# Two layers of chunked attention with a memory and a gated FFN on one core: weight loads moved to SyncE's queue, and the instruction orders built with other margins

## The chip, the cores and the metric

One core of one Trainium2 chip runs the whole program. The metric is device microseconds (us) of one launch, on that core. The kernel before took 537.57 us (median of three runs, 535.77 to 541.40).

## What is computed

The reference works on x of 2048 tokens by 512 channels, in bf16. It does the same two steps twice, with the same weights:

```
x = x + A(layernorm(x), wq, wk, wv, wo, beta)
x = x + B(layernorm(x), w1, w3, w2)
```

A is attention with 32 heads of 16 channels. The 2048 tokens are cut into four segments of 512. Inside a segment every head does causal softmax attention. Beside that, each segment reads a memory that the earlier segments have written:

```
num = phi(qs) @ M ; den = phi(qs) @ z ; a_mem = num / (den + 1e-6)
o   = g * a_mem + (1 - g) * a_dot
M  += phi(ks)^T @ vs ; z += sum over tokens of phi(ks)      # phi(t) = t + 1 for t > 0, else exp(t)
```

with g = sigmoid(beta) of the head, and o @ wo closes the step. B is `(silu(x @ w1) * (x @ w3)) @ w2` with 1376 hidden channels.

## The kernel before, in words

**Segments.** The kernel has eight segment passes, numbered g = 0 to 7 (g = 4 * layer + segment, L949 to L979). A pass normalises its 512 tokens (`layer_norm`), projects q, k and v (`project`), reads the memory (`phi`, `memory_read`; not in segment 0), does the attention (`attention`), writes the memory (`memory_update`; not in segment 3), multiplies by wo and adds (`out_proj`, L878 and L882), normalises again and runs the gated FFN (`ffn`: gate and up products at L909, the down product at L937). All activations and weights stay in SBUF.

**Attention.** The scores of a pass come in 20 units (`unit_list`). A unit is four matmuls of 512 score columns on four row groups of TensorE (L765, "R" work), one exponential on ScalarE (L774, 2048 columns at once, or two of 1024 in pass 0), and causal masks on GpSimd (L787). Later the products with v follow (L813, "C" work), an eviction to `xs` (L448 or L449), a DMA transpose `xg<-xs` on SyncE's queue (L825), the division by the row sums (`normalise`: `rd` at L849 and L848, `og` at L858 or L861), and a DMA transpose `W<-og` (L870) that feeds wo. Pass 0 is done in two halves of 256 tokens, each with its own attention, wo product and second normalisation. Everything else on TensorE is "F" work: projections, wo, FFN.

**Transposes.** The layer norm writes `xn` (L553), and SyncE's queue transposes it into the ring `W` (L557). Transposes of phi(k) (L645) and of `og` go the same way. SyncE's queue carries all 188 DMA transposes.

**The order of the work.** No engine order is written by hand. `Sched` takes all operations with their buffers, priorities and modelled costs, and plays through the program once at build time (`schedule`, L122). For each engine it works out the time s at which each candidate could start: its inputs' modelled ends plus a latency (`_lat`, L117), and the engine's own free time. Candidates within LOOK of the earliest compete by priority. What is picked is appended to that engine's list. The lists are emitted as they are, with semaphore waits (`finalize`, `emit`), so every engine is strictly in order on the chip: where an input is later than the plan thought, the engine stands still, and everything behind it in its list too. A DMA queue is such an engine as well (`sp`, and the issue slots of `act` and `pool`). `gates` hold a candidate back until some other operation is placed in the plan, without a semaphore; `after` adds a real wait.

**The loads.** L493 to L500 issue x tiles 0 to 3, wq, wk and beta from the queues of SyncE and ScalarE. `second_loads` (L502) issues wv from SyncE's queue after the second transpose of pass 0, and x tiles 4 to 7 from GpSimd's queue after the last `lnrs`. `late_loads` (L513) issues the rest from GpSimd's queue, each behind one score unit n of pass 0 (`late`, L510): x tiles 8 to 11 behind unit 1, wo behind 3, w1 and w3 in halves of 688 KB behind 5, 7, 9 and 11, w2 behind 13, 15 and 17, x tiles 12 to 15 behind 18. At the start TensorE runs 28 matmuls on zeros (`WARM`, L475).

Of the kernel before, what the change touches and what calls it, by code (L numbers as in the profile page):

```python
# [8 lines left out]
P = 128  # L9
# [52 lines left out]
class Sched:  # L62
# [53 lines left out]
    @staticmethod  # L116
    def _lat(d, e):  # L117
        if d.dmaq is not None:
            return LAT + (DMA_SLACK if e == "pe" else 0.0)
        return LAT_SAME if d.eng == e else LAT  # L120

    def schedule(self):  # L122
# [15 lines left out]
        xpose_free = 0.0  # L138
# [7 lines left out]
        while left:  # L146
            best = None
            for e in ENGS:
# [3 lines left out]
                for op in avail[e]:  # L152
                    s = max(tf, op.avail_at) if op.gates else tf
# [32 lines left out]
                for s, op in cands:  # L186
                    if s > lim:
                        continue
# [11 lines left out]
            if best is None:  # L200
                held = {}
                for op in self.ops:
                    for b in op.bufs:
                        if b.slot is not None and b.left:
                            held[id(b)] = b
                for b in held.values():
                    print(b.pool.name, b.slot, [(u.name, u.prio) for u in b.users if not u.issued][:3])
                raise RuntimeError("stuck: " + "; ".join(
                    "%s %s" % (op.name, [b.pool.name for b in op.bufs + op.hold if b.slot is None]) for e in ENGS for op in avail[e][:4]))
# [30 lines left out]
            else:  # L240
                if op.mode == "T":
                    x0 = max(s, xpose_free)
                    op.end = x0 + lat + 0.8 * min(max(dma_free - x0, 0.0), 3500.0)
                    xpose_free = x0 + occ
# [3 lines left out]
                else:  # L248
                    x0 = max(s + 700.0, dma_free)
                    dma_free = x0 + op.size / (LOAD_RATE if op.dmaq == "pool" else 300.0)  # L250
# [97 lines left out]
def o_pool(n, per=1.04):  # L348
    return ("pool", 170.0 + per * n, 170.0 + per * n)
# [9 lines left out]
def build(nc, A_x, A_wq, A_wk, A_wv, A_wo, A_beta, B_w1, B_w3, B_w2, out):  # L359
# [81 lines left out]
    def dmaT(fn, **k):  # L441
        return S.add([("sp", 1290.0, 2500.0)], fn, dmaq="sp", mode="T", **k)
# [26 lines left out]
    WARM = 7  # L469
# [32 lines left out]
    def second_loads(first):  # L502
        xt = [op for op in S.ops[first:] if op.name == "xT"]
        ldw("sp", wv_sb, A_wv, "wv", CP + 3, gates=[xt[1]])
        rs = [op for op in S.ops[first:] if op.name == "lnrs"][-1]
        dma("pool", x_tok[:, 4:8, :], xv[:, 4:8, :], 524288, prio=CP + 4, writes=[("x", 4 + j) for j in range(4)], name="ldx",
            gates=[rs], after=[rs])
# [4 lines left out]
    def late_loads():  # L512
        late(x_tok[:, 8:12, :], xv[:, 8:12, :], 524288, 1, [("x", 8 + j) for j in range(4)], "ldx")  # L513
        late(wo_sb[:], A_wo.rearrange("(g p) f -> p g f", p=P), 524288, 3, ["wo"], "ldwo")
        for a in range(2):
            for n, (t, src, key) in enumerate(((w1_sb, B_w1, "w1"), (w3_sb, B_w3, "w3"))):
                late(t[:, 2 * a:2 * a + 2, :], src[256 * a:256 * a + 256, :].rearrange("(g p) f -> p g f", p=P), 704512,
                     5 + 4 * a + 2 * n, [key + str(a)], "ld" + key)
        for a in range(2):
            late(w2_sb[:, 5 * a:5 * a + 5, :], B_w2[640 * a:640 * a + 640, :].rearrange("(t p) d -> p t d", p=P), 655360,  # L520
                 13 + 2 * a, ["w2%d" % a], "ldw2")
        late(w2_sb[0:96, 10, :], B_w2[1280:1376, :], 98304, 17, ["w22"], "ldw2")
# [10 lines left out]
    def layer_norm(s, name, prio, gates=(), fine=False, part=(0, LT), dst=None):  # L533
# [4 lines left out]
        for i in tiles:  # L538
# [3 lines left out]
            dve(lambda e, i=i: e.bn_aggr(ln_r[st.slot][:, i, 6:8], ln_r[st.slot][:, i, 0:6]), 40, reads=[(st, 0, i)],  # L542
                writes=[(st, 1, i)], bufs=[st], prio=prio, name="bnag")
        for a, b in ([(0, 2), (2, 4)] if fine else [part]):
            dve(lambda e, a=a, b=b: e.tensor_scalar(ln_r[st.slot][:, a:b, 8], ln_r[st.slot][:, a:b, 7], 1e-5, None, op0=ALU.add), 20,
                reads=[(st, 1, i) for i in range(a, b)], writes=[(st, 2, i) for i in range(a, b)], bufs=[st], prio=prio, name="lnve")
            pool(lambda e, a=a, b=b: e.tensor_tensor(ln_r[st.slot][:, a:b, 9], ln_r[st.slot][:, a:b, 8], mhalf[:, a:b], ALU.pow), 800,  # L547
                 reads=[(st, 2, i) for i in range(a, b)] + ["mhalf"], writes=[(st, 3, i) for i in range(a, b)], bufs=[st],
                 prio=-1e5 + prio, name="lnrs")
        for i in tiles:  # L550
            tt = 4 * s + i
            xn = new("xn")
            S.add([o_dve(512, False, 1.05)], lambda e, i=i, tt=tt, xn=xn: e.tensor_scalar(  # L553
# [73 lines left out]
    def phi(src, t, dst, dt_, prio, gates=()):  # L627
        for hf in range(2):
# [8 lines left out]
                1024, mode=1.53, reads=[(x, 0), (dst, hf)], writes=[(dst, hf)], bufs=[x, dst], prio=prio, name="phmin")  # L637
# [4 lines left out]
    def memory_update(g, z, pkb):  # L642
# [5 lines left out]
        for hf in range(2):  # L648
            B = new("B")

            def fn(e, hf=hf, B=B):
# [15 lines left out]
                480, reads=[("macc", hf), "bdm"], writes=[(mb, hf)], bufs=[mb], prio=g + 0.3, name="mblk")  # L667
        mstate["mb"] = mb

    def memory_read(g, pqb):  # L670
# [4 lines left out]
        def fn(e):  # L675
            o = None
            for G in range(NCG):
                for i in range(LT):
# [9 lines left out]
                                      gg[:, 0, :][:, None, :].to_broadcast([P, LT, H]), ALU.mult), 128,  # L688
# [139 lines left out]
    def normalise(g, z, part, G, xg, oms):  # L828
# [20 lines left out]
        dve(lambda e: e.reciprocal(rd_r[rd.slot][:, 0, 0:n], sums()), 6.2 * n, reads=[(xg, 0), (xg, 1)], writes=[(rd, 0)],  # L849
            bufs=[xg, rd], prio=pr, name="rd")  # L850
        dve(scaled, n, reads=[(rd, 0), "g1"], writes=[(rd, 1)], bufs=[rd], prio=pr, name="rdg")
        ogv = lambda: og_r[og.slot][:].rearrange("p t (a e d) -> p t a e d", e=2, d=DH)
        for k in range(2):
# [9 lines left out]
            S.add([o_dve(95 * nt), o_pool(64 * nt, 2.25)], fn, reads=[(xg, 0), (xg, 1), (rd, 1)], writes=[(og, k)],  # L863
# [10 lines left out]
    def out_proj(s, g, z, part):  # L874
        for i in range(*part):
            B = new("B")
            for G in range(NCG):
                pe(lambda e, i=i, G=G, B=B: e.matmul(bank(B), ot_r[z.ot.slot][:, G, 128 * i:128 * i + 128], wo_sb[:, G, :],  # L878
                                                     start=(G == 0), stop=(G == NCG - 1)), MM512,
                   reads=[(z.ot, a, i) for a in range(NCG)] + ["wo"], writes=[(B, 0)], bufs=[B, z.ot],  # L880
# [5 lines left out]
    def ffn(s, g, X, part, last=False):  # L886
# [43 lines left out]
        for i in range(t0, t1):  # L930
            B = new("B")
            tt = 4 * s + i
            for ft in range(NFT):
# [5 lines left out]
                    MM512, reads=[(h, 0), "w2%d" % (ft // 5)], writes=[(B, 0)], bufs=[B, h], prio=base + step * n, gates=[prev],  # L939
# [9 lines left out]
    for layer in range(2):  # L949
        for s in range(NS):  # L950
# [16 lines left out]
            if g == 0:  # L967
                later_constants([units[(0, 2)]])
# [47 lines left out]
```

## Time and profile before

| | |
|---|---|
| median of the runs | 537.57 us (535.77 to 541.40) |
| profiled execution, its own time | 541.07 us |
| its span, first to last instruction | 539.2 us, so 1.87 us lie around it |
| mean granted TensorE clock | 0.953 |
| score unit on ScalarE (2048 columns) | 1.88 us, 140 of them |
| gate or up product (512 columns, L909) | 0.388 us latency each, 560 of them |

In the rows, a time is in us from the start of the span; "SPq" is SyncE's DMA queue; the bracket at the end of a timeline row is the idle time of that engine before the instruction and what ended it. PEclk is the granted TensorE clock, 1.00 being full speed. A row of a window gives the busy time of each engine in it, with the number of instructions in round brackets.

### The profile page before, as it was taken

Reading aid. Unit: us, or ns where it says so; the run is one execution under the profiler, and the core shown is the slowest. Engines: PE = TensorE matmul, PEld = TensorE weight load, DVE = VectorE, ACT = ScalarE, POOL = GpSimd, SP = SyncE. Lnnn points to the kernel's source line nnn. Section 1 sums busy time; section 2 is a strip of 40 time slices with the busy share of each in tenths; the row PEclk is TensorE's granted clock in tenths of the full one; section 3 lists DMA queues with packets and bytes.
Section 4 is the critical chain, followed back from the end, with each engine's and each line's share of the span. In section 5 each row is a group of like instructions: output and inputs, shape, how many; then the busy total and the mean of one; then the engine's idle time right before and its main releaser. Section 6 shows DMA issues by size and latency. Waiting matters only on the chain.

```text
span 539.2 us, 10460 instructions
## 1 busy us (share of the span) xinstructions
PE 502.7 (93%) x4180; PEld 218.9 (41%) x4180; DVE 412.1 (76%) x821; ACT 387.2 (72%) x331; POOL 239.1 (44%) x349
## 2 busy tenths in 40 slices
PE   7875997989999999999889999889999999999997
PEld 3431343355455344333334343333333434444443
DVE  5486498888797889677977796989877947777473
ACT  2896687979988989788978798967897877113130
POOL 2685333456554556454534475546654554100000
PEclk9985597989999999999979999999998999999999
DMA  7577653143222314322442034423421141030101
GB/s 189 129 198 173 154 82 78 30 71 80 40 60 42 68 30 89 70 59 51 52 96 50 10 71 68 73 46 56 82 46 34 36 103 41 21 78 1 39 1 39
DMA packets 107200, 36.91 MB, mean 68 GB/s; under 512 B 101296, under 2 KB 105392, under 8 KB 107152
## 3 DMA queue, kind: packets, MB, share of 16 engines
q1 hardware_dynamic: 104640, 29.12, 28.2%
q0 software_dynamic: 1552, 6.32, 4.2%
q8 instruction: 33, 0.54, 0.5%
q10 hardware_dynamic: 960, 0.79, 0.4%
q14 instruction: 15, 0.12, 0.1%
HBM read 8.43 MB, written 2.10 MB: 20 GB/s over the span
## 4 chain that ended last, share of the span: by engine, by line
PE 67%; DVE 16%; DMA 10%; ACT 3%; issue 1%; POOL 1%; SPq 1%; ACTq 0%; DVEq 0%
PE psall L909 26%; PE psall L937 12%; PE psall L765 7%; PE psall L597 6%; PE psall L813 6%; PE psall L878 5%; DMA xg<-xs 3%; PE psall L592 3%; DMA W<-xn 2%; ACT e L774 2%; DMA W<-og 2%; DVE ln L540 1%; DVE xn L553 1%; DVE W L449 1%; DVE W L634 1%; DVE W L636 1%
## 5 line engine op out<-in xcount | busy, mean ns | idle before, releaser
L774 ACT ACTIVATE e<-psall 128x2048 bf16<-128x2048 f32 (+1 forms) x180 | 300.7, 1697 | 57.0 <-PE psall L765 55.3
L787 POOL TENSOR_SCALAR_AFFINE_SELECT e<-e 128x512 bf16<-128x512 bf16 x256 | 164.0, 660 | 165.7 <-ACT e L774 165.5
L909 PE MATMUL psall<-W,w 128*128 128x512 bf16 (+3 forms) x792 | 176.3, 364 | 4.7 <-DVE gp L922 2.4
L909 PEld LDWEIGHTS psall<-W,w 128*128 128x128 bf16 (+1 forms) x792 | 75.2, 102 | 83.6 <-issue 13.8
L920 ACT ACTIVATE th<-psall 128x512 bf16<-128x512 f32 (+2 forms) x89 | 51.6, 591 | 56.9 <-PE psall L909 56.8
L937 PE MATMUL psall<-w,h 128*128 128x512 bf16 (+1 forms) x352 | 85.8, 380 | 0.0
L922 DVE SCALAR_TENSOR_TENSOR gp<-th,psall 128x512 bf16<-128x512 bf16 (+2 forms) x89 | 59.4, 676 | 17.1 <-ACT th L920 16.8
L926 DVE SCALAR_TENSOR_TENSOR h<-gp,psall 128x512 bf16<-128x512 bf16 (+1 forms) x89 | 59.6, 674 | 10.2 <-PE psall L909 9.9
L813 PE MATMUL psall<-e,va 128*32 128x256 bf16 (+3 forms) x1088 | 46.5, 310 | 4.5 <-POOL e L787 2.9
L765 PE MATMUL psall<-W 16*128 16x256 bf16 (+3 forms) x544 | 42.8, 305 | 8.5 <-ACT e L774 7.3
L937 PEld LDWEIGHTS psall<-w,h 128*128 128x128 bf16 (+1 forms) x352 | 32.5, 98 | 38.5 <-issue 4.9
L540 DVE BATCH_NORM_STATS2 ln<-x_tok 128x6 f32<-128x512 bf16 x64 | 43.0, 682 | 1.3 <-DMA x_tok<-in_A_x_dram 0.9
L765 PE MATMUL psall<-W,km 32*128 32x256 bf16 (+3 forms) x544 | 43.1, 307 | 0.4 <-ACT e L774 0.4
L942 DVE TENSOR_TENSOR x_tok<-psall,x_tok 128x512 bf16<-128x512 f32 x32 | 21.9, 685 | 24.8 <-PE psall L937 24.8
L449 DVE CAST xs<-psall 128x512 bf16<-128x512 f32 x56 | 36.7, 681 | 5.4 <-PE psall L813 5.2
L592 PE MATMUL psall<-wv,W 128*128 128x512 bf16 x128 | 36.5, 404 | 4.4 <-DMA wv<-in_A_wv_dram 1.7
L449 DVE CAST W<-psall 128x512 bf16<-128x512 f32 x44 | 29.8, 681 | 11.0 <-PE psall L597 10.9
L597 PE MATMUL psall<-W,wq 128*128 128x512 bf16 (+1 forms) x144 | 35.8, 359 | 1.9 <-DMA W<-xn 1.8
L813 PEld LDWEIGHTS psall<-e,va 128*32 128x32 bf16 x1088 | 24.8, 101 | 28.0 <-POOL e L787 8.2
L597 PE MATMUL psall<-W,wk 128*128 128x512 bf16 (+1 forms) x144 | 36.2, 357 | 0.0
L858 POOL TENSOR_TENSOR og<-xg,rd 128x256 bf16<-128x256 bf16 x33 | 24.6, 750 | 25.4 <-DVE rd L848 21.9
L553 DVE TENSOR_SCALAR xn<-x_tok,ln 128x512 bf16<-128x512 bf16 x64 | 32.5, 531 | 3.6 <-POOL ln L547 3.5
(61 smaller groups left out, 426.9 us busy)
## 6 DMA issues: line engine op xcount, KB each, us to landing
w<-in_B_w_dram POOLq DMA_DIRECT2D x4, 688.0 KB, 5.1
out_dram<-x_tok SPq DMA_DIRECT2D x16, 128.0 KB, 1.7
x_tok<-in_A_x_dram POOLq DMA_DIRECT2D x3, 512.0 KB, 5.6
km<-W SPq DMA_DIRECT2D x24, 64.0 KB, 2.4
w<-in_B_w_dram POOLq DMA_DIRECT2D x2, 640.0 KB, 5.7
W<-xn SPq DMA_TRANSPOSE x64, 2.5
xg<-xs SPq DMA_TRANSPOSE x64, 2.4
W<-og SPq DMA_TRANSPOSE x36, 2.4
```

The lines of the kernel that those rows point to most:

```text
L449: return e.tensor_copy(dst(), src())
L592: fn = lambda e, cg=cg, G=G, B=B, st=st, sp_=sp_: e.matmul(bank(B), xa_r[X.slot][:, cg, 128 * G:128 * G + 128], wv_sb[:, cg, :], start=st, ...
L597: fn = lambda e, cg=cg, G=G, B=B, st=st, sp_=sp_, w=w, a=a, W=W, c0=c0: e.matmul(bank(B)[:, W * a:W * a + W], w[:, cg, 128 * G:128 * G + 1 ...
L765: o = e.matmul(S4[:, sps(pg), c:c + n], kk[32 * pg:32 * pg + r, G, 128 * j:128 * j + 128], q_r[z.q.slot][32 * pg:32 * pg + r, G, 128 * t1 ...
L774: act(lambda e, N=N, ebuf=ebuf, pgs=pgs, sps=sps: e.activation(e_r[ebuf.slot][:, pgs[0]:pgs[-1] + 1, 0:N], S4[:, sps(pgs[0]):sps(pgs[-1]) ...
L787: pool(lambda e, ebuf=ebuf, c=c: e.affine_select(e_r[ebuf.slot][:, :, c:c + 128], e_r[ebuf.slot][:, :, c:c + 128], pattern=[[0, 4], [1, 128]],
L813: o = e.matmul(bank(X)[32 * pg:32 * pg + 32, base + W - n:base + W], va_r[z.va.slot][:, j, h:h + 32], e_r[eb.slot][:, pg, c:c + n], start= ...
L909: prev = pe(lambda e, i=i, cg=cg, ft=ft, B=B, w=w: e.matmul(bank(B)[0:width(ft), W * i:W * i + W], w[:, cg, 128 * ft:128 * ft + width(ft)] ...
L920: act(lambda e, fw=fw, NW=NW, B=B, th=th: e.activation(th_r[th.slot][0:fw, 0:NW], bank(B)[0:fw, 0:NW], ACT.Tanh, scale=0.5), NW, reads=[(B ...
L922: dve(lambda e, fw=fw, NW=NW, B=B, th=th, gp=gp: e.scalar_tensor_tensor(gp_r[gp.slot][0:fw, 0:NW], th_r[th.slot][0:fw, 0:NW], 1.0, bank(B) ...
L926: dve(lambda e, fw=fw, NW=NW, B=B, gp=gps[fg], h=hs[fg]: e.scalar_tensor_tensor(h_r[h.slot][0:fw, 0:NW], gp_r[gp.slot][0:fw, 0:NW], 0.5, b ...
L937: prev = pe(lambda e, ft=ft, fw=fw, B=B, h=h, c=c: e.matmul(bank(B), h_r[h.slot][0:fw, c:c + 128], w2_sb[0:fw, ft, :], start=(ft == 0), st ...
```

## The change

Constants of the planner and its modelled latency:

```diff
-LAT = 60.0
-LAT_SAME = 30.0
-DMA_SLACK = 500.0
-LOAD_RATE = 210.0
+LAT = 150.0
+LAT_SAME = 80.0
+DMA_SLACK = 800.0
+LOAD_RATE = 280.0
...
-LOOK = {"pe": 90.0, "act": 150.0, "dve": 40.0, "pool": 20.0, "sp": 20.0}
+R_SLACK = 0.0
+SLACK = {"pe": 120.0, "act": 0.0, "dve": 200.0, "pool": 60.0, "sp": 0.0}
+LOOK = {"pe": 90.0, "act": 100.0, "dve": 20.0, "pool": 20.0, "sp": 20.0}
...
-            return LAT + (DMA_SLACK if e == "pe" else 0.0)
+            return LAT + (DMA_SLACK if e in ("pe", "dve") else 0.0)
```

So a VectorE instruction that reads a DMA's result is planned 950 ns behind the modelled landing, where it was 60 ns; one on TensorE 950 ns, where it was 560. The candidate's rank now uses w, its input time plus SLACK of the engine (0 for R work), while the planned start stays s:

```diff
-                    cands.append((s, op))
-                    if smin is None or s < smin:
-                        smin = s
+                    w = max(tf, s + (R_SLACK if op.mode == "R" else SLACK[e]))
+                    s = max(tf, s)
+                    cands.append((s, w, op))
+                    if smin is None or w < smin:
+                        smin = w
...
-                for s, op in cands:
-                    if s > lim:
+                for s, w, op in cands:
+                    if w > lim:
```

A transpose is modelled as waiting for all loads that were issued before it, in full:

```diff
-                    op.end = x0 + lat + 0.8 * min(max(dma_free - x0, 0.0), 3500.0)
+                    op.end = x0 + lat + max(dma_free - x0, 0.0)
```

The loads:

```diff
-        xt = [op for op in S.ops[first:] if op.name == "xT"]
-        ldw("sp", wv_sb, A_wv, "wv", CP + 3, gates=[xt[1]])
-        rs = [op for op in S.ops[first:] if op.name == "lnrs"][-1]
-        dma("pool", x_tok[:, 4:8, :], xv[:, 4:8, :], 524288, prio=CP + 4, ..., gates=[rs], after=[rs])
+        ldw("act", wv_sb, A_wv, "wv", CP + 3)
+        rs = [op for op in S.ops[first:] if op.name == "xT"][-1]
+        def early(out_ap, in_ap, size, n, keys, name):
+            dma("sp", out_ap, in_ap, size, prio=CP + 4 + n, writes=keys, name=name, gates=[rs], after=[rs])
+        early(x_tok[:, 4:8, :], xv[:, 4:8, :], 524288, 0, ...)
+        for a in range(2):
+            for n, (t, src, key) in enumerate(((w1_sb, B_w1, "w1"), (w3_sb, B_w3, "w3"))):
+                early(t[:, 2 * a:2 * a + 2, :], src[256 * a:256 * a + 256, :]..., 704512, 2 + 2 * a + n, [key + str(a)], "ld" + key)
```

`late_loads` keeps GpSimd's queue: wo in two halves behind units 5 and 7, x tiles 8 to 11 behind 9, w2 in three pieces of 384 KB behind 11, 13 and 15, its tile 9 behind 16 and its last 96 rows behind 17, x tiles 12 to 15 behind 18. `out_proj` and `ffn` wait for the piece that they read. In pass 0 each token half's two v projections come behind all four q and k products of that half (before: behind the first two), and all of them are gated on the first score unit:

```diff
-                jobs[4 * hf + 2 * hf + 2:4 * hf + 2 * hf + 2] = [("v", (2 * hf,), 0), ("v", (2 * hf + 1,), 0)]
+                jobs += [("v", (2 * hf,), 0), ("v", (2 * hf + 1,), 0)]
...
+                for op in S.ops:
+                    if op.name[0:1] == "v" and op.eng is None and "pe" in op.opts:
+                        op.gates.append(units[(0, 0)])
```

`WARM` goes from 7 to 8, four matmuls more. About ten modelled durations change (`bnag` 40 to 78, `lnve` 20 to 75, `lnrs` 800 to 870, `norm` at 1.45 elements a cycle for 1.05, `phmin` 1.7 for 1.53, `mblk` 480 to 375, `mrg` 128 to 265, `rd` 6.2 to 7.2 a column, `rdg` plus 90, `t2` 95 per tile to 165 + 53 per tile, GpSimd's fixed part 170 to 70 or 115), as does the rate of loads not on GpSimd's queue (300 to 320). The engines' operations stay the same, but for the four warm matmuls. There are 21 loads where there were 19: wo in two instead of one, w2 in five instead of three.

More of the change, by code (lines that the diff above doesn't have):

```diff
@@ L152, in schedule @@
                 for op in avail[e]:
-                    s = max(tf, op.avail_at) if op.gates else tf
+                    s = op.avail_at if op.gates else 0.0
                     for d in op.deps.values():
@@ L200, in schedule @@
             if best is None:
[L201 to L207, printed above, removed]
                 raise RuntimeError("stuck: " + "; ".join(
@@ L348, in o_pool @@
 def o_pool(n, per=1.04):
-    return ("pool", 170.0 + per * n, 170.0 + per * n)
+    return ("pool", 70.0 + per * n, 115.0 + per * n)
 def o_pe(ns):
@@ L512, in late_loads @@
     def late_loads():
-        late(x_tok[:, 8:12, :], xv[:, 8:12, :], 524288, 1, [("x", 8 + j) for j in range(4)], "ldx")
-        late(wo_sb[:], A_wo.rearrange("(g p) f -> p g f", p=P), 524288, 3, ["wo"], "ldwo")
         for a in range(2):
[L516 to L522, printed above, removed]
+            late(wo_sb[:, 2 * a:2 * a + 2, :], A_wo[256 * a:256 * a + 256, :].rearrange("(g p) f -> p g f", p=P), 262144,
+                 5 + 2 * a, ["wo%d" % a], "ldwo")
+        late(x_tok[:, 8:12, :], xv[:, 8:12, :], 524288, 9, [("x", 8 + j) for j in range(4)], "ldx")
+        for a in range(3):
+            late(w2_sb[:, 3 * a:3 * a + 3, :], B_w2[384 * a:384 * a + 384, :].rearrange("(t p) d -> p t d", p=P), 393216,
+                 11 + 2 * a, ["w2%d" % a], "ldw2")
+        late(w2_sb[:, 9, :], B_w2[1152:1280, :], 131072, 16, ["w23"], "ldw2")
+        late(w2_sb[0:96, 10, :], B_w2[1280:1376, :], 98304, 17, ["w23b"], "ldw2")
         late(x_tok[:, 12:16, :], xv[:, 12:16, :], 524288, 18, [("x", 12 + j) for j in range(4)], "ldx")
@@ L862, in fn @@
                                        r[:, :, :, None].to_broadcast([P, nt, 4, DH]), ALU.mult)
-            S.add([o_dve(95 * nt), o_pool(64 * nt, 2.25)], fn, reads=[(xg, 0), (xg, 1), (rd, 1)], writes=[(og, k)],
+            S.add([o_dve(165 + 53 * nt), o_pool(64 * nt, 2.25)], fn, reads=[(xg, 0), (xg, 1), (rd, 1)], writes=[(og, k)],
                   bufs=[xg, og, rd], prio=pr, name="t2")
@@ L879, in out_proj @@
                                                      start=(G == 0), stop=(G == NCG - 1)), MM512,
-                   reads=[(z.ot, a, i) for a in range(NCG)] + ["wo"], writes=[(B, 0)], bufs=[B, z.ot],
+                   reads=[(z.ot, a, i) for a in range(NCG)] + ["wo%d" % (G // 2)], writes=[(B, 0)], bufs=[B, z.ot],
                    prio=g + 0.9 + 0.001 * i - 900, name="o%d" % i)
```

39 lines of the change are left out of this document (20 added, 19 removed).

## The prediction

> **What bounds the kernel now.** I read the page first, for the shares of the engines.
>
> ```profile
> span 539.2 us, 10460 instructions
> PE 502.7 (93%) x4180; PEld 218.9 (41%) x4180; DVE 412.1 (76%) x821; ACT 387.2 (72%) x331; POOL 239.1 (44%) x349
> PEclk9985597989999999999979999999998999999999
> ```
>
> TensorE is counted busy for 93% of the span, but the clock row shows a hole in slices 3 to 5 (8, 5, 5 tenths) and a few small ones later. So the second view is busy time and clock by stage.
>
> ```profile
> core 0: us, PE busy (x) PEld busy (x) DVE busy (x) ACT busy (x) POOL busy (x), PEclk, DMA share, GB/s
> 13.00:27.00 14.00, 12.17 (x141) 5.64 (x141) 6.99 (x13) 11.33 (x15) 8.28 (x13) 1.00 0.56 130
> 27.00:36.00 9.00, 6.72 (x97) 3.06 (x95) 6.38 (x18) 9.00 (x11) 6.99 (x12) 0.97 0.64 188
> 36.00:66.00 30.00, 23.16 (x200) 7.63 (x199) 19.75 (x51) 21.00 (x23) 15.79 (x23) 0.50 0.76 176
> 66.00:135.00 69.00, 61.32 (x622) 32.39 (x621) 58.57 (x119) 57.22 (x50) 31.51 (x47) 0.92 0.39 68
> 135.00:458.00 323.00, 311.29 (x2722) 129.56 (x2720) 263.61 (x515) 270.57 (x206) 169.62 (x243) 0.98 0.31 57
> 458.00:539.20 81.20, 77.81 (x361) 35.62 (x358) 49.96 (x85) 15.51 (x26) 3.37 (x4) 1.00 0.11 30
> ```
>
> The last 81.2 us are almost pure TensorE work: ScalarE has 15.51 us to do, GpSimd 3.37. That is FFN and output work put off from earlier passes. So TensorE sets the end, and each microsecond in which it idles or runs at half clock before 458 us is paid there. The worst stage is 36 to 66 us: 23.16 us busy at clock 0.50 are 11.6 us of full-speed work in 30. The other 18.4 us are the most that this stage can give back. From 27 to 36 ScalarE is busy for all of its 9.00 us, so there the exponentials set the pace and TensorE has nothing else to do. From 66 to 458 TensorE idles 7.68 + 11.71 = 19.4 us, and the clock costs 61.32 x 0.08 + 311.29 x 0.02 = 11.1 us more.
>
> Third, the chain of waits and the timeline in the bad stage: what is TensorE short of?
>
> ```profile
> 27.41 5.37 DMA xg<-xs
> 39.12 5.14 DMA xg<-xs
> 46.95 5.05 DMA W<-og
> 52.05 1.46 PE psall L878 x3
> ```
> ```profile
> 32.81 0.25 DVE L849 RECIPROCAL rd<-xg 128x16 f32<-128x16 bf16 x1 [2.62 <-DMA xg<-xs]
> 43.76 1.76 SPq L825 DMA_TRANSPOSE xg<-xs  x1
> 44.28 0.25 DVE L849 RECIPROCAL rd<-xg 128x16 f32<-128x16 bf16 x1 [0.54 <-DMA xg<-xs]
> 45.23 0.51 POOL L861 TENSOR_TENSOR og<-xg,rd 128x128 bf16<-128x128 bf16 x1 [0.99 <-DVE rd L848]
> 45.70 0.69 POOL L787 TENSOR_SCALAR_AFFINE_SELECT e<-e 128x512 bf16<-128x512 bf16 x1
> 48.00 1.68 PE L813 MATMUL psall<-e,va 128*32 128x256 bf16 x32 [2.92 <-POOL e L787]
> 49.74 0.60 ACT L448 ACTIVATE xs<-psall 128x512 bf16<-128x512 f32 x1 [3.49 <-PE psall L813]
> ```
>
> Three transposes in a row on the chain take 5.05 to 5.37 us. VectorE's list stands at the reciprocal that reads one (2.62 us idle), GpSimd stands behind VectorE (0.99), a mask comes late, TensorE stands at the attention product (2.92) and ScalarE behind that (3.49). This is a late input that holds four in-order engines one after another. What makes the transposes slow shows in the DMA rows, the whole run first, then 27 to 54 us.
>
> ```profile
> w<-in_B_w_dram POOLq DMA_DIRECT2D x4, 688.0 KB, 5.1
> xg<-xs SPq DMA_TRANSPOSE x64, 2.4
> ```
> ```profile
> xg<-xs SPq DMA_TRANSPOSE x5, 5.1
> W<-og SPq DMA_TRANSPOSE x5, 4.0
> ```
>
> 2.4 us over the run, 5.1 while w1 and w3 come in. So a transpose that meets a load costs about 2.7 us more.
>
> **The change, part by part.** *wv on ScalarE's queue.* At the start TensorE stands for wv:
>
> ```profile
> 12.35 0.60 PE L597 MATMUL psall<-W,wq 128*128 128x256 bf16 x4
> 13.18 0.35 DVE L615 TENSOR_SCALAR km<-W,cm 128x512 bf16<-128x512 bf16 x1 [2.22 <-ACT W L448]
> 14.66 1.04 PE L592 MATMUL psall<-wv,W 128*128 128x512 bf16 x4 [1.71 <-DMA wv<-in_A_wv_dram]
> 16.23 5.60 ACT L774 ACTIVATE e<-psall 128x1024 bf16<-128x1024 f32 x6
> ```
>
> The scores need only `km`, done at 13.53, but stand in the list behind the v product. With wv in time, and v behind the first unit, the first exponential starts near 14.2: 2.0 us gained. Against it stands that wv shares the engines with the first transposes. Half a megabyte takes 1.45 us at the start's rate:
>
> ```profile
> 3.00:6.00 3.00, 3.00 (x11) 1.17 (x10) 1.84 (x6) 1.13 (x1) 0.45 (x1) 1.00 1.07 361
> ```
>
> so the bounds are +2.0 and -1.5; I take +1.5, since x tiles 2 and 3 stay ahead of wv. beta comes 1.45 us later and delays only its own tanh; the four warm matmuls lie in the idle time before the first projection. Both count nothing.
>
> *x tiles 4 to 7, w1 and w3 on SyncE's queue.* SyncE waits for the last first-pass transpose to land, then issues five loads. What stands behind them on the queue is the first `xg<-xs`:
>
> ```profile
> SPq L825 <- DVE xs L449: 11.8, 1, 11.8
> ```
> ```profile
> 9.37 0.58 SPq L439 DMA_DIRECT2D wv<-in_A_wv_dram  x1
> 10.67 2.50 SPq L557 DMA_TRANSPOSE W<-xn  x2
> 24.94 3.67 SPq L825 DMA_TRANSPOSE xg<-xs  x2
> ```
>
> The queue is idle for 11.8 us here. Five issues of 0.58 are 2.9 us, and the wait for the landing is some 2.5 to 5 us (the ends of the transposes above) from 13.2: done by about 21, before the transpose is due at 23 to 25. Issue is hidden. The data are 0.52 + 4 x 0.70 = 3.34 MB. At 361 GB/s they take 9.3 us and end near 26; at the 188 of the mixed stage 17.8 us, ending near 34. An estimate between them, nearer to the first because nothing else is in flight, is 28. So the first pair of transposes may land 0 to 8 us late; I take 1.5. The gain is that the later ones no longer meet w1 and w3.
> The rule that speaks against this part is in the Trainium skill, "DMA: Bandwidth & Descriptors", section "Queues, rings and completion order": SP's DMAs share one ring per DMA engine, consumed in order, while different queues take turns packet by packet. By that rule the first transposes would wait for all the loads, not share with them. The trace of before cannot show it, because its only load between SyncE's transposes is wv; by the rule the delay is the end of the loads, by the rows above 26 to 34, and the sum would lose up to 8 us in place of 1.5.
>
> Three chain transposes at 2.4 in place of 5.05 to 5.37 are 5.37 + 5.14 + 5.05 - 3 x 2.4 = 8.4 us. The loads that stay on GpSimd's queue are smaller pieces, 3.0 MB in all for 5.8 MB behind the units before, so about half the collisions remain: I take 5.5 of 8.4. The hold of VectorE, GpSimd, TensorE and ScalarE above goes with them, and it is in the chain already. But the wo product then comes some 6 us sooner, while the clock is at half: the same time at 0.50 is worth half as much in work, so that the clock must come back sooner too. It came back when TensorE got dense projections:
>
> ```profile
> 63.00:66.00 3.00, 3.00 (x8) 1.06 (x7) 1.01 (x2) 1.75 (x2) 1.18 (x2) 0.50 0.42 134
> 66.00:69.00 3.00, 3.00 (x48) 1.89 (x47) 1.76 (x4) 1.54 (x2) 0.15 (x1) 0.97 0.75 90
> ```
>
> I shift that point by the chain, and count the shift once: 5.5 us, less the 1.5 of the first pair. Bounds: -4 (loads in the way) to 18.4 (no hole).
> That the weights come earlier is worth nothing by itself:
>
> ```profile
> L909 PE MATMUL psall<-W,w x792: 270/379/634, 107.8 to 525.9; 128*128 128x512 bf16 x140, 128*128 128x256 bf16 x38, 128*96 128x512 bf16 x14, 128*96 128x256 bf16 x6
> 38.63 0.72 POOL L439 DMA_DIRECT2D w<-in_B_w_dram  x1 [0.31 <-PE psall L765]
> ```
>
> The last of w1 and w3 was issued at 38.63 and its FFN first ran at 107.8. That gap covers w2 in pieces as well. wo, split and behind units 5 and 7, has until 52.05. x tiles 8 to 11 move from unit 1 to unit 9: the norm that reads them stood at about 40 us, so up to 2 us of VectorE are at risk; VectorE has 10.25 us idle from 36 to 66, so I count nothing. Three fewer GpSimd issues at 0.72 are 2.2 us of an engine that is busy half of that stage: nothing.
>
> *The margins.* They add and remove nothing; they move readers of DMAs down VectorE's list by 0.89 us and those on TensorE by 0.39, and all cross-engine readers by 0.09 to 0.29. Gain: holds such as 2.62, 0.54 and 0.99 above, and TensorE's 19.4 us of idle time and 11.1 of clock from 66 to 458. Cost: results taken later than they could be. Bounds: +30.5 (all of it) to -10.7 (the last rival). Nothing in the trace prices it; I take 8, a quarter of what is there, because the hold chain shows the fault that margins answer, but ScalarE and VectorE are 83 to 85% busy from 66 to 135 and leave little room.
>
> **The sum**, against the profiled execution (541.07, that is the span and 1.87 around it): 1.5 + 5.5 - 1.5 + 8 = 13.5, so 527.6. That execution lies 3.5 above the median of 537.57. The same gain on the median gives 524.
>
> **The rivals.** *The clock hole closes.* If projections of pass 1 reach TensorE before the clock falls at about 35 us, most of the 18.4 go. For it: VectorE, which makes their input, loses 2.62 us in just that stretch to a late transpose. Against it: TensorE had only 6.72 of 9.00 us of work there, with ScalarE full. Three quarters of 18.4 in place of the 5.5 - 1.5 give 541.07 - 1.5 - 13.8 - 8 = 517.8, on the median 514.
> The Trainium skill ("TensorE: Matmul & The Clock Gate", "The HAM clock gate") has the clock fall after an idle window of about 3.4 us and come back after a busy one; the rise after dense work at 63 to 66 agrees, the fall at 36 does so only if sparse score work counts as idle.
> *Hidden anyway.* ScalarE is full until 45 us with or without late transposes, no weight was waited for but wv, and a new list only moves the holes. Then 1.5 and some 2 to 3 us of chain remain: 541.07 - 4 = 537, on the median 534; half of this case is within 1%.
> *Slower: readers behind the margin.* VectorE's `rd` now stands 0.89 us behind the planned landing, plus 0.09 to `og`, and the wo product 0.39 behind its transpose's old place: 1.2 us more for each of nine attention parts (two in pass 0, one in each other). It decides where TensorE has no other work. There the clock falls too, as here:
>
> ```profile
> 80.90:94.40 13.50, 10.13 (x112) 5.19 (x111) 11.34 (x25) 9.70 (x7) 4.54 (x8) 0.75 0.38 78
> ```
>
> Idle 3.37 and 2.53 of clock, 5.9 us for one such hole. Nine parts cost 10.7 us; with the start's gain and no other, 541.07 + 10.7 - 1.5 = 550.3, on the median 547. It decides from the point where it eats the 1.5 and the 4.0 of the start and the chain: five of the nine parts.
>
> **How the numbers follow.** Chances: forecast 0.42, clock hole closes 0.20, hidden anyway 0.18, slower 0.20. A measurement of this kernel can tell about 1% from no change. Faster takes the first two and half of the third, less a little of the forecast's own spread: 0.65; same 0.16; slower 0.19. The forecast's own range is 516 to 532. To hold 8 in 10 the whole range goes from 504 (the closed hole and twice the margins' gain: 514 - 8, and 2 of spread) to 545 (short of the slower rival's full price).
>
> **What would show it.** Right: no wait on wv, first exponential near 14 us; `xg<-xs` near 2.4 to 3.5 us between 30 and 54; the first wo product near 46 in place of 52; the clock back before 60; less TensorE idle time from 66 to 458. Wrong: the first `xg<-xs` landing after 32 us with VectorE standing at `rd`; new rows of TensorE waiting over 2 us for `og` or the norm; clock below 0.9 in stages where it was 1.00.

## The result, and the profile after

The changed kernel takes 516.58 us (median of four runs, 515.98 to 517.81) where the kernel before took 538.18 in the same comparison: ratio 0.9598, 95% interval 0.9543 to 0.9652. That is 21.6 us faster; 13.5 was forecast. The profiled execution took 515.98 us with a span of 514.2. The page of the kernel after:

```profile
span 514.2 us, 10399 instructions
PE 484.8 (94%) x4117; PEld 215.5 (42%) x4184; DVE 403.1 (78%) x809; ACT 396.1 (77%) x350; POOL 229.7 (45%) x340
PEclk9987999999999999999889999999999999999999
```

The hole in the clock row, slices of 8, 5 and 5 tenths before, is now one of 8 and one of 7; two slices near 250 us stand at 8. The same stages as in the prediction, of the kernel after:

```profile
13.00:27.00 14.00, 13.88 (x168) 6.86 (x168) 10.82 (x21) 13.21 (x16) 9.70 (x16) 1.00 0.96 272
27.00:36.00 9.00, 6.06 (x83) 2.23 (x86) 8.89 (x26) 9.00 (x12) 7.28 (x11) 0.99 0.55 147
36.00:66.00 30.00, 25.47 (x285) 10.75 (x278) 23.04 (x57) 28.04 (x30) 17.49 (x27) 0.83 0.83 154
66.00:135.00 69.00, 63.94 (x660) 33.35 (x665) 59.11 (x122) 63.42 (x57) 35.21 (x52) 1.00 0.33 62
135.00:458.00 323.00, 311.69 (x2645) 132.57 (x2691) 259.01 (x504) 269.77 (x220) 156.43 (x227) 0.99 0.29 58
458.00:514.20 56.20, 52.39 (x239) 24.07 (x242) 35.24 (x62) 10.14 (x17) 1.02 (x1) 1.00 0.10 29
```

For each stage I add TensorE's idle time and its busy time times one minus the clock. From 13 to 27 us 1.8 became 0.1; from 36 to 66 us 18.4 became 8.9 (4.53 idle, 4.33 clock); from 66 to 135 us 12.6 became 5.1; from 135 to 458 us 17.9 became 14.4. At 458 us TensorE had 77.81 us of work left before and 52.39 after: it had done 25.4 us more by then, which is the gain of 25.0 in the span. (That the window from 458 us on is 25.0 us shorter shows nothing by itself, since it begins at the same time in both.) The clock column has two digits, and in the kernel after 46 matmuls of the long stage have no record (2645 for 2691 weight loads), so that some of its idle time may be work. The long stage is good to some 5 us only, and 14.4 is if anything too much.

At the start, in the timeline after, the scores stand ahead of v, and the first exponential comes 1.7 us sooner than at 16.23:

```profile
14.13 0.25 PE L766 MATMUL psall<-W 16*128 16x128 bf16 x4
14.57 8.36 ACT L775 ACTIVATE e<-psall 128x1024 bf16<-128x1024 f32 x9 [0.51 <-PE psall L766]
14.82 1.03 PE L593 MATMUL psall<-wv,W 128*128 128x512 bf16 x4
```

SyncE's queue in the kernel after, then the DMA rows of 13 to 27 us, then those of 27 to 54 us:

```profile
14.79 2.17 SPq L436 DMA_DIRECT2D w<-in_B_w_dram  x4
21.98 10.50 SPq L826 DMA_TRANSPOSE xg<-xs  x4
```
```profile
w<-in_B_w_dram SPq DMA_DIRECT2D x4, 688.0 KB, 8.1
xg<-xs SPq DMA_TRANSPOSE x2, 4.4
```
```profile
W<-og SPq DMA_TRANSPOSE x5, 4.7
xg<-xs SPq DMA_TRANSPOSE x4, 4.1
```

Two things are to be seen. The first transposes, issued behind the loads on the same queue, took 4.4 us, 2.0 more than the 2.4 of the whole run before, but they were issued 3 us sooner than before. And the later transposes are not quick: 4.1 and 4.7 us, where the prediction wanted 2.4 to 3.5. The first wo product came at 45.44 in place of 52.05 all the same, and the clock came back some 20 us sooner, near 46 us (chain, then windows, of the kernel after):

```profile
14.57 13.45 ACT e L775 x15
29.84 5.51 ACT e L775 x6
37.94 3.72 ACT e L775 x4
45.44 1.33 PE psall L879 x4
```
```profile
45.00:48.00 3.00, 2.84 (x21) 0.82 (x15) 2.49 (x5) 2.38 (x3) 1.80 (x2) 0.81 0.63 96
48.00:51.00 3.00, 3.00 (x24) 0.88 (x24) 3.00 (x9) 3.00 (x4) 2.05 (x4) 1.00 1.10 232
```

The chain shows the largest difference. Before, three transposes of `xs` and `og` made 15.56 us of it between 27 and 52 us. Now it runs mostly over ScalarE's exponentials until 42 us, and the next transpose on it is one of the norm, at 50.38 us. The transposes did not get quick; they left the chain.

### The profile page after: what moved, and what is told of

Same layout as the page of the kernel before. It is cut to its first block, busy times and chain, and to the rows that moved or that the text cites. A ratio compares the mean times of both kernels' runs of the same rounds, so it can differ in the third digit from the quotient of the medians.

```text
span 514.2 us, 10399 instructions
## 1 busy us (share of the span) xinstructions
PE 484.8 (94%) x4117; PEld 215.5 (42%) x4184; DVE 403.1 (78%) x809; ACT 396.1 (77%) x350; POOL 229.7 (45%) x340
## 4 chain that ended last, share of the span: by engine, by line
PE 69%; DVE 17%; ACT 7%; DMA 4%; issue 2%; POOL 0%; ACTq 0%; DVEq 0%
PE psall L910 25%; PE psall L938 15%; PE psall L598 7%; PE psall L766 7%; ACT e L775 6%; PE psall L814 6%; PE psall L879 4%; DVE xn L554 3%; PE psall L593 3%; DMA W<-xn 2%; DVE h L927 2%; DVE ln L541 2%; DVE gp L923 2%; DVE W L446 1%; DVE W L637 1%
## 5 line engine op out<-in xcount | busy, mean ns | idle before, releaser
L910 PE MATMUL psall<-W,w 128*128 128x512 bf16 (+3 forms) x768 | 168.1, 357 | 3.7 <-issue 1.6
L910 PEld LDWEIGHTS psall<-W,w 128*128 128x128 bf16 (+1 forms) x792 | 73.8, 100 | 78.6 <-issue 13.5
L938 PE MATMUL psall<-w,h 128*128 128x512 bf16 (+1 forms) x338 | 83.8, 380 | 1.3 <-issue 0.6
L923 DVE SCALAR_TENSOR_TENSOR gp<-th,psall 128x512 bf16<-128x512 bf16 (+2 forms) x89 | 59.2, 672 | 12.8 <-ACT th L921 12.6
L766 PE MATMUL psall<-W,km 32*128 32x256 bf16 (+3 forms) x544 | 41.7, 297 | 0.1
L554 DVE TENSOR_SCALAR xn<-x_tok,ln 128x512 bf16<-128x512 bf16 x64 | 34.8, 574 | 4.0 <-DMA W<-xn 2.0
L598 PE MATMUL psall<-W,wq 128*128 128x512 bf16 (+1 forms) x141 | 34.7, 356 | 0.7 <-DMA W<-xn 0.4
L598 PE MATMUL psall<-W,wk 128*128 128x512 bf16 (+1 forms) x139 | 34.5, 356 | 0.3 <-issue 0.2
L593 PE MATMUL psall<-wv,W 128*128 128x512 bf16 x118 | 32.4, 383 | 1.8 <-issue 1.0
L766 PEld LDWEIGHTS psall<-W 16*128 16x128 bf16 x544 | 13.2, 92 | 48.6 <-ACT e L775 41.8
L879 PE MATMUL psall<-wo,W 128*128 128x512 bf16 x117 | 30.0, 384 | 1.0 <-issue 0.6
```

What stands on the lines that cost most here:

```text
L598: fn = lambda e, cg=cg, G=G, B=B, st=st, sp_=sp_, w=w, a=a, W=W, c0=c0: e.matmul(bank(B)[:, W * a:W * a + W], w[:, cg, 128 * G:128 * G + 1 ...
L766: o = e.matmul(S4[:, sps(pg), c:c + n], kk[32 * pg:32 * pg + r, G, 128 * j:128 * j + 128], q_r[z.q.slot][32 * pg:32 * pg + r, G, 128 * t1 ...
L910: prev = pe(lambda e, i=i, cg=cg, ft=ft, B=B, w=w: e.matmul(bank(B)[0:width(ft), W * i:W * i + W], w[:, cg, 128 * ft:128 * ft + width(ft)] ...
L923: dve(lambda e, fw=fw, NW=NW, B=B, th=th, gp=gp: e.scalar_tensor_tensor(gp_r[gp.slot][0:fw, 0:NW], th_r[th.slot][0:fw, 0:NW], 1.0, bank(B) ...
L938: prev = pe(lambda e, ft=ft, fw=fw, B=B, h=h, c=c: e.matmul(bank(B), h_r[h.slot][0:fw, c:c + 128], w2_sb[0:fw, ft, :], start=(ft == 0), st ...
```

## The experiments

I split the change into three: **loads** (all moved and cut DMAs, the place of the v projections, eight warm-up groups), **margins** (LAT, LAT_SAME, DMA_SLACK, SLACK, LOOK and the ranking by w), and **durations** (the modelled costs, load rates, and the model of a transpose behind loads). Six kernels, with the two that were there, make all eight combinations. The theory of the prediction: loads and planner each give a part, and the loads own the stage up to 66 us. The rival: the planned order does it. All ratios are against the kernel before.

**e1_loads**, the kernel before with the loads of the diff in `second_loads`, `late_loads`, `project` and `WARM`:

```diff
-        ldw("sp", wv_sb, A_wv, "wv", CP + 3, gates=[xt[1]])
+        ldw("act", wv_sb, A_wv, "wv", CP + 3)
...
+            dma("sp", out_ap, in_ap, size, prio=CP + 4 + n, writes=keys, name=name, gates=[rs], after=[rs])
```

> The kernel before with the loads alone changed: wv on ScalarE's queue, x tiles 4 to 7, w1 and w3 on SyncE's, wo and w2 in pieces, the v projections behind the first score unit, eight warm-up groups; planner constants and modelled durations as before. Theory (the stage up to 66 us belongs to the loads, the rest to the planner): the profile after saved about 2 us up to 36 us and 9.6 us from 36 to 66, so this kernel takes 538 - 10 to 12 = 526 to 528, with the clock back near 46 to 50 us, and 66 to 458 us as before (19 us of idle time). Rival (the planner did it all): 535 to 539, with the clock low from 36 to beyond 60 us.

Measured: 533.86 us, ratio 0.9896 (0.9817 to 0.9974). A gain of some 5.6 us, between the theory's 526 to 528 and the rival's 535 to 539, and not the stage that the theory gave to the loads. The stage 36 to 66 us in e1_loads, and its timeline:

```profile
36.00:66.00 30.00, 22.30 (x195) 7.71 (x190) 17.56 (x44) 18.53 (x21) 13.68 (x20) 0.55 0.82 118
```
```profile
46.78 1.68 PE L817 MATMUL psall<-e,va 128*32 128x256 bf16 x32 [4.33 <-DMA W<-xn]
48.51 0.60 ACT L448 ACTIVATE xs<-psall 128x512 bf16<-128x512 f32 x1 [4.90 <-PE psall L817]
49.36 0.76 POOL L439 DMA_DIRECT2D w<-in_B_w_dram  x1 [5.23 <-PE psall L769]
49.42 0.25 DVE L853 RECIPROCAL rd<-xg 128x16 f32<-128x16 bf16 x1 [5.10 <-DMA xg<-xs]
```

Without margins the order again lets late transposes stop four engines, here for 4.3 to 5.2 us each. (TensorE waits for the transposed norm that the v projection of pass 1 reads; its weight load stands in the list ahead of the matmul shown.) Moving the loads did not remove such a hold; the next late input made another.

**e2_margins**, the kernel before with the margins alone:

```diff
-LAT = 60.0
-LAT_SAME = 30.0
-DMA_SLACK = 500.0
+LAT = 150.0
+LAT_SAME = 80.0
+DMA_SLACK = 800.0
...
+                    w = max(tf, s + (R_SLACK if op.mode == "R" else SLACK[e]))
```

> The kernel before with the margins alone: LAT, LAT_SAME, DMA_SLACK (VectorE too), SLACK and LOOK as in the changed kernel; loads and modelled durations as before. Theory (margins answer late inputs after 66 us, where the profile after has 2.6 us less idle time and 8 us less lost clock): 538 - 6 to 9 = 529 to 532. Rival (readers behind the margin come too late): 543 to 548. Second rival (margins are nothing without durations that are right): 536 to 540.

Measured: 527.79, ratio 0.9784 (0.9697 to 0.9872), below the theory's 529 to 532 and far from the rival that margins come too late.

**e3_durations**, the kernel before with the modelled costs alone:

```diff
-    return ("pool", 170.0 + per * n, 170.0 + per * n)
+    return ("pool", 70.0 + per * n, 115.0 + per * n)
...
-                    op.end = x0 + lat + 0.8 * min(max(dma_free - x0, 0.0), 3500.0)
+                    op.end = x0 + lat + max(dma_free - x0, 0.0)
```

> The kernel before with the modelled durations alone: the ten operation costs, GpSimd's fixed part, the load rates, and transposes that wait for all earlier loads in full. Theory (the margins do the planner's part): 535 to 540, no change. Rival (durations nearer to the measured ones do it): 528 to 532.

Measured: 540.59, ratio 0.9997 (0.9952 to 1.0042): nothing, as expected.

**e4_planner**, margins and durations together, the loads of the kernel before:

```diff
+LAT = 150.0
+SLACK = {"pe": 120.0, "act": 0.0, "dve": 200.0, "pool": 60.0, "sp": 0.0}
...
         ldw("sp", wv_sb, A_wv, "wv", CP + 3, gates=[xt[1]])
```

> The kernel before with margins and durations, loads as before. Theory (two parts that add): 538 - 11 = 527, with the hole from 36 to 66 us as in the kernel before and less idle time and less lost clock from 66 to 458 us. Rival (the planner did it all): 517 to 520. Rival (the loads are what makes it work): 535 to 539.

Measured: 520.83, ratio 0.9658 (0.9587 to 0.9729). This is next to the rival's 517 to 520: the order gives most of the gain without a single load moved. The hole from 36 to 66 us shrank too, which the theory did not expect. In e4_planner the stage, the DMA rows of 27 to 54 us, and the first dense product after the gap with the first wo product:

```profile
36.00:66.00 30.00, 26.82 (x288) 11.53 (x292) 22.52 (x63) 27.22 (x30) 15.15 (x23) 0.77 0.89 187
```
```profile
xg<-xs SPq DMA_TRANSPOSE x5, 3.9
W<-og SPq DMA_TRANSPOSE x5, 4.3
```
```profile
43.72 1.06 PE L589 MATMUL psall<-wv,W 128*128 128x512 bf16 x2 [0.33 <-issue]
50.38 0.82 PE L875 MATMUL psall<-wo,W 128*128 128x512 bf16 x3
```

The transposes meet w1 and w3 and are about as slow as in the kernel after, but the projections of pass 1 start at 43.72 in place of 57.4, and the half clock ends near 49 us. What the late transposes fed was put behind other work: before, the wo product (52.05) stood ahead of these projections, and here (50.38) it stands behind the first of them.

**e5_fill_before and e6_fill_after** ask whether the half clock itself is the price. The order is that of the kernel before (e5) and after (e6); ahead of each half unit's scores in the second half of pass 0 stand two dense matmuls into the same banks, whose results are overwritten (56 more matmuls):

```diff
                         o = None
+                        if g == 0 and pi == 1:
+                            for pg in pgs:
+                                e.matmul(S4[:, sps(pg), :], wq_sb[:, pg, 0:128], wk_sb[:, pg, :], start=True, stop=True)
```

> The kernel before with its order unchanged, and two dense matmuls of 512 columns, thrown away, ahead of the score matmuls of each half unit in the second half of pass 0 (56 matmuls, 12 us of TensorE at full clock, into the score banks that are overwritten at once). They add work and remove no wait. Theory (the half clock from 36 to 66 us is most of the price of the hole): the clock stays at 1.00 from 27 to 66 us, the 11.6 us of lost clock come back, less up to 4 us where the added matmuls delay scores: 538 - 8 = 530 (527 to 533). Rival (the clock follows the hole but the late transposes set the time): 537 to 543.

> The changed kernel with the same 56 thrown-away matmuls. Theory: the hole from 36 to 46 us is filled, the 4.3 us of lost clock come back less 1 to 2 us: 516.6 - 3 = 513.5. Rival: 517 to 520.

Measured: e5 535.71, ratio 0.9955 (0.9925 to 0.9985); e6 522.25, ratio 0.9707 (0.9647 to 0.9767), so 5.7 us slower than the changed kernel and outside both of its forecasts. In e5_fill_before the stage, and the first wo product:

```profile
36.00:66.00 30.00, 27.43 (x276) 9.99 (x280) 21.60 (x57) 25.81 (x28) 17.85 (x27) 1.00 0.96 202
```
```profile
54.09 0.82 PE L881 MATMUL psall<-wo,W 128*128 128x512 bf16 x3 [0.16 <-DMA W<-og]
```

The clock is 1.00 throughout, and yet the wo product comes no sooner than at 52.05 and the kernel gains 0.45%, not the 8 us expected. The added matmuls cost TensorE time and delay scores, so this is no clean price of the clock. But it shows that a full clock did not bring the stage's inputs sooner: the chain that leads to 60 us still passes through three transposes of `xs` and `og`, of 5.53, 2.69 and 5.34 us. How much a full clock without the added work would give stays open.

**e7_loads_margins and e8_loads_durations**, the changed kernel without the durations, and without the margins. The edits are those of e3 and e2 taken back:

```diff
-    return ("pool", 70.0 + per * n, 115.0 + per * n)
+    return ("pool", 170.0 + per * n, 170.0 + per * n)
...
```
```diff
-LAT = 150.0
+LAT = 60.0
...
-                    w = max(tf, s + (R_SLACK if op.mode == "R" else SLACK[e]))
```

> The changed kernel without the modelled durations: loads and margins only. If the parts add: 538 x 0.9896 x 0.9784 = 521. If the durations matter only under margins, as the planner pair (520.8) against margins alone (527.8) suggests: 522 to 525, so 6 to 8 us above the changed kernel.

> The changed kernel without the margins: loads and modelled durations only. If the margins are the term that counts: 531 to 536, as with the loads alone. Rival (the durations work with the loads, since a transpose is planned behind all loads): 522 to 527.

Measured: e7 523.28, ratio 0.9726 (0.9660 to 0.9792); e8 531.04, ratio 0.9854 (0.9780 to 0.9928). So e7 came where durations matter only under margins, and e8 at the edge of where margins are the term that counts. With these, each part can be compared four times, with the others there or not:

| part | change of the time, four pairs | mean |
|---|---|---|
| margins | -2.2, -1.7, -3.4, -2.6% | -2.5%, 13 us |
| loads | -1.0, -0.6, -1.4, -0.6% | -0.9%, 5 us |
| durations | 0.0, -0.4, -1.3, -1.3% | -0.8%, 4 us |

The pairs run from the part alone to the part on top of both others. They are worked out from the ratios above, each of which has an interval of 0.4 to 0.9% to either side, so a pair is good to about 1%. Margins are clear of zero in all four pairs; loads in two, alone and with durations only; durations in the two with margins, which give 1.3% each. How far the order itself scatters is a second question, and the control below bears on it.

The same eight kernels by stage, each number being TensorE's idle time and what the clock cost, in us, as above:

| kernel | 36 to 66 us | 66 to 458 us |
|---|---|---|
| before | 18.4 | 30.5 |
| loads (e1) | 17.7 | 33.3 |
| margins (e2) | 16.5 | 27.4 |
| durations (e3) | 18.1 | 36.3 |
| margins and durations (e4) | 9.3 | 24.2 |
| loads and margins (e7) | 10.9 | 24.4 |
| loads and durations (e8) | 8.5 | 36.6 |
| all three (after) | 8.9 | 19.5 |

No part alone closes the hole from 36 to 66 us, and any two close about half of it, without margins too. The row of e8:

```profile
36.00:66.00 30.00, 26.89 (x275) 10.60 (x277) 23.73 (x61) 25.77 (x26) 16.86 (x26) 0.80 0.83 139
```

It loses as little there as the changed kernel, and yet takes 531.04 us, only 2.8 less than e1 with its open hole, which is not clear of zero. So the hole is not by itself what the margins win. Their part shows behind it: with margins 8.9, 12.1 and 17.1 us less are lost from 66 to 458 us (e7 to e1, e4 to e3, after to e8). This column is good to some 5 us. In it the kernel before can't be held against the others, since all of them lack 40 to 47 matmul records there and it lacks none.

**e9 to e12** take the margins apart, in the changed kernel, and hold against them a control:

```diff
-SLACK = {"pe": 120.0, "act": 0.0, "dve": 200.0, "pool": 60.0, "sp": 0.0}
+SLACK = {"pe": 0.0, "act": 0.0, "dve": 0.0, "pool": 0.0, "sp": 0.0}
```


> The changed kernel with SLACK zero on every engine: candidates are ranked by their modelled input time again; latencies, DMA slack, durations and loads as changed. If ranking is the part of the margins that counts: back towards loads and durations without margins (531), so 525 to 531. If longer latencies are what counts: 515 to 519.

```diff
-            return LAT + (DMA_SLACK if e in ("pe", "dve") else 0.0)
+            return LAT + (DMA_SLACK if e == "pe" else 0.0)
```


> The changed kernel with DMA_SLACK for TensorE's readers alone: VectorE's readers of transposes are planned 0.15 us behind the modelled landing in place of 0.95. If VectorE held by late transposes is what the margins answer, as the prediction had it: 521 to 527, with rows of VectorE waiting at rd for the transpose. If the 0.95 only costs time (the prediction's slower rival): 512 to 515. Else 516 to 519.

```diff
-LAT = 150.0
-LAT_SAME = 80.0
+LAT = 60.0
+LAT_SAME = 30.0
```


> The changed kernel with the old latencies, 60 ns between engines and 30 ns on one. If longer latencies are the part that counts: 524 to 531. If the ranking is: 515 to 519.

```diff
-LAT = 150.0
-LAT_SAME = 80.0
+LAT = 140.0
+LAT_SAME = 75.0
```


> The changed kernel with latencies of 140 and 75 ns for 150 and 80: a control. It says how far any other order of the same kind moves the time. If orders of one kind agree: 515 to 519. If each is a draw of its own: 510 to 524, and then differences below that between single kernels say nothing of the constant that was changed.

Measured: e9 536.21, ratio 0.9942 (0.9906 to 0.9978); e10 528.45, ratio 0.9840 (0.9794 to 0.9887); e11 525.23, ratio 0.9776 (0.9738 to 0.9813); e12, the control, 527.76, ratio 0.9822 (0.9782 to 0.9862). e9 is slower than either of its forecasts, and e12 lies outside both of its own. The control is the run that changes how the others are read: 10 and 5 ns of assumed latency move the kernel by 11 us; they change nothing but the order of the lists. So e10 and e11, which land within 3 us of the control, show nothing of VectorE's DMA slack or of the longer latencies. e9 alone stands off from the control, by 8.4 us; it is even slower than e8, which has no margins at all. That is one order against one, and no more than the control itself moved, so it points at the ranking without proving it.

An estimate from these runs says what the scatter does to the table of parts. The four kernels that keep loads, durations and the ranking slack (516.58, 525.23, 527.76 and 528.45) have a standard deviation of 5.5 us. If each order is a draw of that width, a mean of four pairs is uncertain by 5.5 over the square root of 2, some 4 us. The 13 us of the margins stand clear of that; the 5 of the loads and the 4 of the durations do not.

The stages of e9:

```profile
36.00:66.00 30.00, 26.53 (x249) 10.24 (x242) 19.74 (x47) 23.24 (x24) 14.90 (x25) 0.59 0.61 132
66.00:135.00 69.00, 59.30 (x579) 29.65 (x585) 61.62 (x121) 56.84 (x46) 34.37 (x49) 0.93 0.33 64
```

Without the slack in the ranking the clock stays low from 36 to 66 us and TensorE idles 9.70 us from 66 to 135. The second is as in e8 without margins (10.07); the first is not, since the clock was 0.80 there in e8. The control keeps the first stage and loses later. Its windows, and one of the kernel after for comparison:

```profile
66.00:135.00 69.00, 61.19 (x629) 29.98 (x634) 61.53 (x123) 60.25 (x49) 36.78 (x53) 0.95 0.34 63
330.00:395.00 65.00, 58.05 (x541) 24.58 (x543) 54.01 (x104) 53.73 (x43) 30.77 (x45) 1.00 0.31 60
```
```profile
330.00:395.00 65.00, 63.04 (x540) 25.74 (x547) 53.54 (x103) 56.07 (x46) 32.22 (x48) 1.00 0.26 52
```

Idle time of 7.81 us in place of 5.06 with some clock lost, and of 6.95 in place of 1.96: the holes sit where this order happens to have them.

## Why the prediction was right, and where it was not

**The direction and the bound** held. What TensorE wins before the end, it need not do at the end: 25.4 us less of its work was left at 458 us, and the span is 25.0 us shorter.

**The start** was sized 1.5 us. From 13 to 27 us TensorE's idle time fell from 1.83 to 0.12, and the first exponential came 1.7 us sooner. About right.

**The loads** were sized 5.5 us in all (1.5 + 5.5 - 1.5). Alone they give 5.6, on average of four pairs 5. The size came out; the working did not, and beside a scatter of 5.5 us the agreement may be luck. It had the three transposes of the chain down to about 3.4 us each (5.5 of 8.4 us won). They stayed at 4.1 and 4.7, with w2, wo and x still coming in beside them, and in the changed kernel they left the chain instead. What the loads alone show is the start (first exponential at 14.33, 1.9 us sooner) and a first wo product at 49.86 in place of 52.05; where the rest of their 5 us comes from stays open, and with a control that moves by 11 us single pairs do not settle it. GpSimd issues two loads fewer (nine for eleven), not three as the prediction has it; nothing hangs on that.

**The loads ahead of the transposes.** Taken as a loss of 1.5 us, with 8 as the bound. The first transposes took 2.0 us more than the undisturbed 2.4, and they had been issued 3 us sooner; the first reciprocal that reads one came at 28.21 in place of 29.15 us, so there was no loss against the kernel before. The ring order that the Trainium skill gives ("DMA: Bandwidth & Descriptors", "Queues, rings and completion order") agrees with 4.4 us behind loads of the same queue. But the 5.1 us beside GpSimd's loads in the kernel before were no better, so for a transpose that meets a load the queue made little difference here.

**The margins** are the term that was mis-sized: 8 us, where margins alone give 11.7 and their four pairs 13. The prediction put their gain at 66 to 458 us, and that step holds: in the changed kernel the idle time there fell from 19.4 to at most 16.4 us and the clock's cost from 11.1 to 3.1, and the pairs give 8.9 to 17.1. What it had wrong is the stage before. It gave 36 to 66 us to the loads, at 4.0 us net. There 9.5 came back, and no part alone gives more than 1.9; it takes two of the three, and the order alone (e4) brings the projections of pass 1 forward from 57.4 to 43.72 us. It also took modelled durations as nothing by themselves, which holds (e3), without seeing that they work under the margins (1.3%).

The reason given, late inputs that hold engines, is borne out in part: by e1 (holds of 4.3 to 5.2 us where the margins are missing) and e4 (equally slow transposes, a shorter hole). But VectorE itself still stands for a transpose. Its waits from 24 to 66 us, before and after:

```profile
DVE rd L849 <- DMA xg<-xs: 3.2, 2, 2.6
```
```profile
DVE rd L850 <- DMA xg<-xs: 3.1, 1, 3.1
```

What went is the rest of the hold: the longest waits of TensorE's matmuls and of ScalarE in that stretch fell from 2.9 and 3.5 us to 1.1 each. That it is VectorE's DMA slack that does it is not shown: e10 cannot be told from the control.

**The rivals.** The closed hole came half true: of 18.4 us in that stage 9.5 came back, where the forecast had 4.0 and this rival 13.8, and the measured 516.58 lies nearer to its 514 than to the forecast's 524. But e5 and e8 show that a full clock, or a hole closed as far as here, gains little by itself: 0.45% with the added matmuls in the way, and 0.4% from e1 to e8. Hidden anyway is out: loads alone moved little, but the whole moved 4%. Readers behind the margin is out as a net effect: e2, with margins alone, is 2.2% faster. (Its price was also added up wrong: 0.89, 0.09 and 0.39 make 1.37 us, not 1.2, and so 12.3 for nine parts, not 10.7.)

**The signs.** The first exponential, the first wo product, the clock and the idle time came as the prediction said; `xg<-xs` at 4.1 us did not come to 2.4 to 3.5. No wait of a TensorE matmul for `og` or the norm is over 2 us; the longest of all is 1.3. The clock stands at 8 tenths near 250 us, where the kernel before has one slice of 7 near 276.

**What may be luck.** The changed kernel is 8.7 to 11.9 us faster than its three neighbours that keep the ranking slack (525.23, 527.76, 528.45; in the first and the last a constant of the margins is taken back). Their mean, 527.1, is a gain of 11, and the forecast was 13.5. So the whole 8 us by which the forecast fell short may be that this order is a good draw among its kind. Against that, margins and durations together are worth 17 us on the mean of the pairs. Three neighbours and one order for each combination are too few to settle it.

## What to carry to other kernels

Where a program lists every in-order engine's work ahead of time, the plan's assumed input times can matter more than the transfers (here 13 us against 5): rank work as if its inputs came a little late, and use durations read from a trace with it. Judge a constant of such a planner by several kernels on each side, or at least beside a control that moves it a little; one comparison of two orders says only which of the two is faster. In this kernel the low clock was first a sign that inputs were missing: filling the gap with idle work lifted the clock, and the time fell by 0.45% in one kernel and rose by 1.1% in the other.

## What the runs showed of the hardware beyond that

In the kernel before, TensorE was counted busy without a gap from 54 to 66 us and the clock stayed at 0.50 (one window of that stretch, then the row of the timeline that ends it):

```profile
54.00:57.00 3.00, 3.00 (x14) 0.51 (x13) 1.94 (x3) 2.05 (x2) 0.64 (x1) 0.50 1.22 252
```
```profile
62.72 3.59 PE L592 MATMUL psall<-wv,W 128*128 128x512 bf16 x8
```

The Trainium skill ("TensorE: Matmul & The Clock Gate", "The HAM clock gate") has the clock return after about 3.4 us of sustained work. Here score, attention, wo and v matmuls by turns did not bring it back from 54 to 62.7 us, all of it counted busy, so the busy column is not what the gate sees. The eight v matmuls in a row from 62.72 fit the page: 3.59 us of them, and the clock is 0.97 from 66 to 69. TensorE's clock stayed at 1.00 through 27 to 66 us with two matmuls of 512 columns added to each half unit (e5), where it was 0.50 from 36 to 66 us without them. Loads issued in a row on SyncE's queue, with nothing issued beside them, moved 392 GB/s in the kernel after, more than the 361 that the prediction used:

```profile
18.00:21.00 3.00, 3.00 (x48) 1.63 (x46) 2.26 (x5) 3.00 (x5) 2.91 (x6) 1.00 1.02 392
```
